# Batch 0 of a Fourier layer and a maxout layer on one core: the complex weight product by three products instead of four

## The chip, the core and the metric

The kernel runs on one core of one Trainium2 chip. The metric is the device time of one execution in microseconds (us). Before the change three runs took 1979.61, 1980.62 and 1983.82 us, median 1980.62. TensorE (PE) does the matmuls, VectorE (DVE) and ScalarE (ACT) the work between them, GpSimd (POOL) mostly issues DMAs, and SyncE (SP) only issues DMAs.

## The reference, cut to what matters

The input x has 8 batches of 3072 x 256. Each batch goes through a Fourier layer and then a maxout layer:

```python
X = np.fft.rfft(x, axis=1)                      # 3072 long
Yr = Xr @ w_r - Xi @ w_i + b_r                  # the complex product, 256 x 256
Yi = Xr @ w_i + Xi @ w_r + b_i
Y = soft_threshold(Yr) + 1j * soft_threshold(Yi)   # |.| - 0.01, not below 0
y = np.fft.irfft(Y, n=3072, axis=1)
h = np.maximum(np.maximum(y @ w1, y @ w2), y @ w3) # 256 -> 768
out = h @ w_out                                    # 768 -> 256
```

The maxout weights arrive as float64 and are turned into pairs of float16 numbers (a high and a low part) on the chip, with a common power of two that needs the largest magnitude of all of them.

## The kernel before, in words

The transform of length 3072 = 96 x 32 is done in two steps. A first product over 96 (`stage_a`, tile `pa`) writes to `a_d` in DRAM. Then come 12 groups, k = 0 to 11, each with four of the 48 pairs of frequencies: a second product over 32 (`stage_b`, tile `px`, result `t`), the complex weight product (`stage_w`, tile `py`, result `u`), the soft threshold, and the first product of the inverse (`stage_q`, tile `pz`, copied to `zs` and stored to `z_d`). When all 12 groups of a batch are in `z_d`, it is read back in eight chunks (`load_z`, tile `zq`) and the last inverse product (`pi`) and the maxout layer (`up`, tile `pu`; `down`, tile `pd`) follow.

Batches 1 to 7 are prepared while the maxout layer of the batch before them runs, in float16 pairs. Batch 0 has nothing to hide behind. It runs ahead of everything in plain float32 (`first_b`, `first_w`, `first_q`), in a loop k = -3 to 12 that does in this order: load `aj` of group k + 3, `first_b(k + 1)`, `first_w(k)`, `finish_w(k)`, `first_q(k - 1)` with its store, and then the items of `plan[k]`.

The plan prepares the maxout weights beside the groups. `load` brings a pair of tiles (SP), `largest` takes a maximum (DVE), `scale` finds the common exponent (DVE and a small matmul `pt`), and four phases `exponent`, `combine`, `join` and `finish` (DVE and ACT by turns, tiles `rw`, `ru`, `xhl`, `wuh`, `wul`, `woh`, `wol`) turn a tile into its float16 pair. `w_up` is the three input weights, `w_dn` is w_out. `w_dn.load(4)` is in `plan[6]`, `w_dn.largest(4)` and `w_dn.scale` in `plan[7]`. Later phases of other tiles are issued by `pump` from k = 8 on, and more behind the loop.

Every engine works through its instructions in a fixed order, which the compiler's scheduler chose: it follows the program, but puts an instruction ahead where its inputs are expected to be ready. So the plan's instructions stand between those of the groups, some before the program's place. SP issues `aj`, the weights, the tables and x's tiles in one queue; ACT issues `z_d` of batch 0 (L894); POOL issues `a_d`, the output, and `z_d` of other batches.

In `first_w` before the change `t` holds for each half j of the group (64 columns) the columns [-imag, real, imag]. Each half takes two products with w_r and two with w_i, over two blocks of the 256 inputs: 8 float32 matmuls of 128 x 256, with both halves' real and imaginary parts as rows 0 to 63 and 64 to 127. DVE adds the bias (L696), ACT makes the two one-sided parts (L701, L702), DVE subtracts them (L703). `first_q` needs the real rows of a half on partitions 0 to 63 and its imaginary rows on 64 to 127, which is how `u` lies. Group 11 has special frequencies and its own tables.

Of the kernel before, what the change touches and what calls it, by code (L numbers as in the profile page):

```python
# [101 lines left out]
def fourier_maxout_kernel(  # L102
# [131 lines left out]

    def load_fft_weights():
# [16 lines left out]
    def load_last_bias():  # L252
        rows = [b.rearrange("(r o d) -> r o d", r=1, o=1) for b in (b_r, b_i)]
        for c in range(2):
            nc.sync.dma_start(out=bias[64 * c:64 * c + 64, 1:2], in_=rows[c].broadcast_to([64, 1, D]))
        nc.gpsimd.dma_start(out=bias[96:97, 1:2], in_=rows[0])
# [53 lines left out]
    def scale_bias():  # L310
        mb = small("mxb")
        nc.vector.tensor_reduce(
            out=mb, in_=bias[:, 0], axis=AX.X, op=ALU.max, apply_absolute_value=True
# [191 lines left out]
    def load_m(q):  # L505
        b, q4 = divmod(q, NCH)
        xv = x[b].rearrange("(n1 n2) d -> n1 n2 d", n2=N2)[:, q4 * NQ:(q4 + 1) * NQ, :]
        with tc.issue_after(st["ld"].ins):
            st["m", q] = xm = fft.tile([N1, NQ * D], F32, name="xm", bufs=1)
# [148 lines left out]
    def first_b(k):  # L658
# [8 lines left out]
        st["t", k] = t = fft.tile([P, KD, 384], F32, name="tf", tag="t2", bufs=2)  # L667
        tv = t.rearrange("p h (j m) -> p (h j) m", j=2)
# [12 lines left out]

    def first_w(k):
        last = k == NJP - 1
# [3 lines left out]
        for j in range(2):  # L687
# [12 lines left out]
        t = fft.tile([P, 2, D], F32, name="t", bufs=1)  # L700
        nc.scalar.activation(out=t, in_=u, func=AF.Relu, bias=mlam)  # L701
        nc.scalar.activation(out=u, in_=u, func=AF.Relu, scale=-1.0, bias=mlam)  # L702
        nc.vector.tensor_tensor_reduce(  # L703
            out=u, in0=u, in1=t, scale=1.0, scalar=0.0, op0=ALU.subtract, op1=ALU.max,
            accum_out=mx[:, NJP + k:NJP + k + 1],
        )
# [4 lines left out]
        st["u", k] = u  # L711

    def first_q(k):
        u = st.pop(("v", k))
        pz = ff_tile("pz")
# [163 lines left out]
    def stage_q(k):  # L879
        b, kb = divmod(k, NJP)  # L880
        if b == 0 or plain(k):
# [11 lines left out]
            for q in range(2):  # L893
                nc.scalar.dma_start(  # L894
# [257 lines left out]
    for k in range(-3, NJP + 1):  # L1152
        for fn, i in (
            (load_a, k + 3), (stage_b, k + 1), (stage_w, k), (finish_w, k), (stage_q, k - 1),
        ):
            if 0 <= i < NJP:
                if fn == stage_q and i == NJP - 1:
# [4 lines left out]
        with tc.issue_after(st["ld"].ins):  # L1162
# [15 lines left out]
            if k == 6:  # L1178
                whole = ga_sb.rearrange("p i e n m -> p (i e n m)")
                nc.sync.dma_start(out=whole, in_=ga[:, 0:2 * N2 * N1])  # L1180
                first = fft.tile([N1, NQ * D], F32, name="xm", bufs=1).bitcast(F16)[:, 0:2 * NT]
# [8 lines left out]
    with tc.issue_after(st["late"].ins):  # L1190
        for c, v in enumerate((b_r, b_i)):
            row = v.rearrange("(o d) -> o d", o=1)
# [104 lines left out]
```

## Time and profile before

| | before |
|---|---|
| median of three runs | 1980.62 us |
| the profiled execution's own time | 1980.65 us |
| its span in the trace | 1978.9 us |
| PE busy over the span | 1961.3 us (99%) |
| DVE busy | 1521.3 us (77%) |
| ACT busy | 1064.3 us (54%) |
| POOL busy | 280.5 us (14%) |
| mean granted TensorE clock | 0.998 |

Busy time is the union of an engine's instructions; issuing a DMA is not counted as busy. A row of a timeline has its start, the time from the start of its first to the end of its last instruction, the engine, the line of the kernel, the operation, the tiles, and in square brackets the idle time of the engine before it and what ended that. Instructions of one engine overlap at their ends, so the step from one start to the next is what an instruction costs its engine. A float32 matmul stands as two records. Groups 0 to 11 of batch 0 lie between about 27 and 98 us of the span; the first maxout matmul starts at 110.78 us.

### The profile page before, as it was taken

How to read it: one execution, taken by the hardware profiler on the slowest of the kernel's cores; microseconds unless marked ns; L12 is line 12 of the kernel's file. 1: busy time of each engine (PE TensorE's matmuls, PEld its weight loads, DVE VectorE, ACT ScalarE, POOL GpSimd, SP SyncE). 2: the span in 40 equal slices, each digit the busy share in tenths (PEclk: the TensorE clock that was granted, in tenths of full speed). 3: DMA queues.
4: the chain of work that ended last, by engine and by line, in shares of the span. 5: the costliest groups of instructions: out<-in, count | busy, mean ns of one | idle time of the engine just before them, and what ended most of it. 6: DMA issues, size and time to landing. Idle time of an engine off the chain costs nothing.

```text
span 1978.9 us, 44328 instructions
## 1 busy us (share of the span) xinstructions
PE 1961.3 (99%) x16839; PEld 1355.9 (69%) x16839; DVE 1521.3 (77%) x3159; ACT 1064.3 (54%) x2186; POOL 280.5 (14%) x510
## 2 busy tenths in 40 slices
PE   9989999999999999999999999999999999999999
PEld 5746776676766766666766676666676677766666
DVE  3788887888877988778887888868887687765554
ACT  5755664566545565456554565545655455443343
POOL 1001111111111122111121021111122001100000
PEclk9999999999999999999999999999999999999999
DMA  8756564565545564555555465544552344221111
GB/s 291 212 150 172 157 163 124 156 174 154 145 133 163 143 189 115 151 150 161 159 137 149 133 186 145 147 139 130 149 154 73 90 115 123 68 76 49 49 49 33
DMA packets 201843, 269.75 MB, mean 136 GB/s; under 512 B 30846, under 2 KB 149982, under 8 KB 201534
## 3 DMA queue, kind: packets, MB, share of 16 engines
q1 hardware_dynamic: 168830, 191.37, 36.7%
q0 software_dynamic: 25168, 68.59, 10.7%
q10 hardware_dynamic: 7632, 6.95, 1.2%
q8 instruction: 133, 2.18, 0.5%
q14 instruction: 80, 0.66, 0.1%
HBM read 124.31 MB, written 75.50 MB: 101 GB/s over the span
## 4 chain that ended last, share of the span: by engine, by line
PE 93%; DVE 3%; DMA 2%; ACT 1%; issue 1%; SPq 0%; ACTq 0%; DVEq 0%
PE pu L179 19%; PE pu L181 18%; PE pu L180 18%; PE pd L181 6%; PE pd L180 6%; PE pd L179 6%; PE py L179 3%; PE py L180 3%; PE py L181 3%; PE pi L1021 2%; PE px L737 2%; PE pa L575 2%; PE pz L905 1%; PE pa L592 1%; PE py L692 0%
## 5 line engine op out<-in xcount | busy, mean ns | idle before, releaser
L179 PE MATMUL pu<-yh,wuh 128*128 128x384 f16 x2304 | 752.2, 327 | 2.6 <-DVE h L1062 1.7
L181 PE MATMUL pu<-yh,wul 128*128 128x384 f16 x2304 | 751.5, 326 | 0.0
L180 PE MATMUL pu<-yl,wuh 128*128 128x384 f16 x2304 | 751.5, 326 | 0.0
L173 ACT ACTIVATE hh<-h 128x384 f16<-128x384 f32 x384 | 200.2, 521 | 432.3 <-DVE h L1062 428.4
L181 PEld LDWEIGHTS <-wul 128*128 128x128 f16 x2304 | 225.5, 98 | 149.7 <-issue 0.9
L179 PEld LDWEIGHTS <-wuh 128*128 128x128 f16 x2304 | 225.3, 98 | 145.1 <-issue 34.2
L181 PE MATMUL pd<-woh,hh 128*128 128x256 f16 x1152 | 313.4, 273 | 0.7 <-DVE hh L174 0.7
L180 PE MATMUL pd<-wol,hh 128*128 128x256 f16 x1152 | 313.8, 273 | 0.0
L179 PE MATMUL pd<-woh,hh 128*128 128x256 f16 x1152 | 313.8, 273 | 0.0
L180 PEld LDWEIGHTS <-wuh 128*128 128x128 f16 x2304 | 225.5, 98 | 116.1 <-issue 5.0
L174 DVE SCALAR_TENSOR_TENSOR hh<-h,hh 128x384 f16<-128x384 f32 x384 | 213.3, 555 | 108.3 <-ACT hh L173 105.4
L1059 DVE TENSOR_TENSOR c<-pu,c 128x384 f32<-128x384 f32 x384 | 212.1, 552 | 95.8 <-PE pu L181 90.3
L1056 ACT ACTIVATE c<-pu 128x384 f32<-128x384 f32 x384 | 186.7, 486 | 139.9 <-PE pu L181 136.8
L1062 DVE TENSOR_TENSOR h<-pu,c 128x384 f32<-128x384 f32 x384 | 211.7, 551 | 29.2 <-PE pu L181 24.8
L1093 POOL DMA_DIRECT2D out_dram<-o x189 | 104.7, 559 | 581.3 <-ACT o L1091 569.7
L585 POOL DMA_DIRECT2D a_d<-aq x160 | 94.0, 591 | 612.4 <-ACT aq L582 590.0
L181 PE MATMUL py<-wch,tt 128*128 128x256 f16 x504 | 137.3, 273 | 0.0
L179 PE MATMUL py<-wch,tt 128*128 128x256 f16 x504 | 137.3, 272 | 0.0
L180 PE MATMUL py<-wcl,tt 128*128 128x256 f16 x504 | 137.3, 272 | 0.0
L179 PEld LDWEIGHTS <-hh 128*128 128x128 f16 x1152 | 112.7, 98 | 33.5
L180 PEld LDWEIGHTS <-hh 128*128 128x128 f16 x1152 | 112.7, 98 | 33.4
L181 PEld LDWEIGHTS <-hh 128*128 128x128 f16 x1152 | 112.7, 98 | 15.2 <-DVE hh L174 1.9
(236 smaller groups left out, 2659.3 us busy)
## 6 DMA issues: line engine op xcount, KB each, us to landing
zq<-z_d SPq DMA_DIRECT2D x63, 384.0 KB, 4.8
out_dram<-o POOLq DMA_DIRECT2D x189, 128.0 KB, 3.3
ab<-a_d SPq DMA_DIRECT2D x84, 256.0 KB, 4.1
ab<-ab SPq DMA_DIRECT2D x336, 64.0 KB, 3.0
vb<-vb SPq DMA_DIRECT2D x308, 64.0 KB, 2.9
z_d<-zs POOLq DMA_DIRECT2D x70, 256.0 KB, 3.8
xm<-in_x_dram SPq DMA_DIRECT2D x40, 384.0 KB, 3.5
a_d<-aq POOLq DMA_DIRECT2D x160, 96.0 KB, 2.9
```

The costliest lines, as they stand in the source:

```text
L173: nc.scalar.activation(out=hi, in_=src, func=AF.Copy, scale=scale)
L174: later(lambda: low(nc.vector.scalar_tensor_tensor(out=lo, in0=src, scalar=scale, in1=h, op0=ALU.mult, op1=ALU.subtract)))
L179: nc.tensor.matmul(o, lh, rh, start=start, stop=False, **kw)
L180: nc.tensor.matmul(o, lh, rl, start=False, stop=False, **kw)
L181: st["mm"] = nc.tensor.matmul(o, ll, rh, start=False, stop=stop, **kw)
L575: st["mm"] = nc.tensor.matmul(pa[r][64 * h:64 * h + 64], ft[rows, t], xt[rows, i, h], start=t == i, stop=t == 1,)
L585: nc.gpsimd.dma_start(out=av[1 - r, :, :, n:n + 512], in_=o[64 * h:64 * h + 48])
L737: nc.tensor.matmul(pv[:, h, :, g // 2, g % 2], ah[:, g // 2, g % 2, h * P:(h + 1) * P], mb_sb[:, i, 4 * kb + g].rearrange("p (c m) -> p c ...
L1056: st["act"] = nc.scalar.activation(out=c1, in_=p, func=AF.Copy)
L1059: st["dve"] = nc.vector.tensor_tensor(out=c1, in0=p, in1=c1, op=ALU.max)
L1062: st["dve"] = nc.vector.tensor_tensor(out=h32, in0=p, in1=st["c1"], op=ALU.max)
L1093: q.dma_start(out=out_v[b, c, t], in_=o)
```

## The change

For groups 0 to 10 the complex product is made by three products. With R and I the real and imaginary inputs, c = (R + I) w_r, then Yr = c - I (w_r + w_i) and Yi = c + R (w_i - w_r). `t` now holds R, I and their sum for all 128 frequencies of a group (ACT copies R and I, DVE adds them), the two sums of the weights are made once by DVE, and `first_w` becomes `quick_w`: 6 float32 matmuls of 128 x 256 in two PSUM tiles, a DVE addition of c and the bias (`bias_ri`, both biases side by side on all partitions), and a DVE addition of the other two products that also takes the maximum. The threshold is as before.

The result lies with real and imaginary parts side by side and 128 frequencies on the partitions, so four DMAs on SP of 64 rows each (64 KB) move the rows of `u` to `moved` in the order that `first_q` needs. `first_q` now runs two groups behind (`k - 2`, was `k - 1`); groups 10 and 11 both follow at k = 12. `z_d` of groups 0 to 9 is issued by POOL instead of ACT. `w_dn.largest(4)` and `w_dn.scale` stand in `plan[8]` instead of `plan[7]`. `bias_ri` is loaded early on SP in place of the first half of `bias`; its late load on POOL is gone. `moved` uses the buffers of `aq`, the weights' sums part of the tile `xm`.

```diff
+    spare_x = fft.tile([P, NQ * D], F32, name="xm", bufs=1)
+    sums = spare_x[:, 2 * D:4 * D].rearrange("p (k d) -> p k d", k=KD)
+    def sum_fft_weights(ws):
+        for kd, t in enumerate(ws):
+            r, i, s = (t[:, n * D:n * D + D] for n in range(3))
+            nc.vector.scalar_tensor_tensor(
+                out=sums[:, kd], in0=r, scalar=-1.0, in1=i, op0=ALU.mult, op1=ALU.subtract
+            )
+            nc.vector.tensor_tensor(out=s, in0=i, in1=r, op=ALU.subtract)
...
-            nc.sync.dma_start(out=bias[64 * c:64 * c + 64, 0:1], in_=rows[c].broadcast_to([64, 1, D]))
+            nc.sync.dma_start(out=bias_ri[:, c:c + 1], in_=rows[c].broadcast_to([P, 1, D]))
...
+        if k < NJP - 1:
+            pc = px.rearrange("p (h j c m) -> p h c j m", h=KD, j=2, c=2)
+            for c in range(2):
+                nc.scalar.activation(
+                    out=t[:, :, c * P:c * P + P].rearrange("p h (j m) -> p h j m", j=2), in_=pc[:, :, c],
+                    func=AF.Copy,
+                )
+            nc.vector.tensor_tensor(
+                out=t[:, :, 2 * P:3 * P], in0=t[:, :, 0:P], in1=t[:, :, P:2 * P], op=ALU.add
+            )
+            return
...
+    def quick_w(k):
+        t = st.pop(("t", k))
+        mx = batch(0, "u")
+        both = [ff_tile("py") for _ in range(2)]
+        for o, part, w in (
+            (both[0][:, 0:D], 2, [v[:, 0:D] for v in fft_weights]),
+            (both[1][:, 0:D], 1, [sums[:, h] for h in range(KD)]),
+            (both[1][:, D:2 * D], 0, [v[:, 2 * D:3 * D] for v in fft_weights]),
+        ):
+            for h in range(KD):
+                nc.tensor.matmul(
+                    o, t[:, h, part * P:(part + 1) * P], w[h], start=h == 0, stop=h == KD - 1
+                )
+        u = fft.tile([P, 2, D], F32, name="uf", tag="vh", bufs=3)
+        nc.vector.tensor_tensor(
+            out=u, in0=both[0][:, 0:D].rearrange("p (o d) -> p o d", o=1).broadcast_to([P, 2, D]),
+            in1=bias_ri, op=ALU.add,
+        )
+        nc.vector.tensor_tensor_reduce(
+            out=u, in0=both[1].rearrange("p (c d) -> p c d", c=2), in1=u, scale=1.0, scalar=0.0,
+            op0=ALU.add, op1=ALU.max, accum_out=mx[:, k:k + 1],
+        )
+        first_threshold(k, u)
+        if k % 2 == 0:
+            st["moved"] = fft.tile([P, NQ * D], F32, name="aq", bufs=2)
+        st["mv", k] = moved = st["moved"][:, k % 2 * 512:k % 2 * 512 + 512].rearrange("p (j d) -> p j d", j=2)
+        for c in range(2):
+            for j in range(2):
+                nc.sync.dma_start(out=moved[64 * c:64 * c + 64, j], in_=u[64 * j:64 * j + 64, c])
...
-                nc.scalar.dma_start(
+                (nc.gpsimd if k < NJP - 2 else nc.scalar).dma_start(
...
-    for k, n in ((4, 0), (5, 2), (5, 3), (7, 4)):
+    for k, n in ((4, 0), (5, 2), (5, 3), (8, 4)):
         planned(k, w_dn.largest, n)
-    planned(7, w_dn.scale)
+    planned(8, w_dn.scale)
...
-            (load_a, k + 3), (stage_b, k + 1), (stage_w, k), (finish_w, k), (stage_q, k - 1),
+            (load_a, k + 3), (stage_b, k + 1), (stage_w, k), (finish_w, k), (stage_q, k - 2),
+            (stage_q, NJP - 1 if k == NJP else -1),
```

## Rows read from the trace of the kernel before

**Rows 1.** The page's first two parts: busy time of the engines over the span, and DVE's busy share in 40 equal slices of 49.5 us (tenths, 9 is 90% or more).

```profile
span 1978.9 us, 44328 instructions
PE 1961.3 (99%) x16839; PEld 1355.9 (69%) x16839; DVE 1521.3 (77%) x3159; ACT 1064.3 (54%) x2186; POOL 280.5 (14%) x510
...
DVE  3788887888877988778887888868887687765554
```

**Rows 2.** Busy time by stretches: start and end, length, then busy us (and instructions) of PE, PEld, DVE, ACT and POOL, the granted clock, the mean busy share of the 16 DMA engines, and GB/s. The third row of stretches is from the bias addition of group 0 to that of group 11.

```profile
34.99:73.53 38.54, 36.90 (x187) 30.23 (x186) 34.58 (x85) 28.34 (x49) 0.49 (x1) 1.00 0.97 311
73.53:93.64 20.11, 20.11 (x99) 16.58 (x98) 15.42 (x42) 15.63 (x27) 1.54 (x5) 1.00 0.61 158
34.99:93.64 58.65, 57.01 (x285) 46.81 (x284) 50.00 (x125) 43.98 (x75) 2.03 (x6) 1.00 0.85 258
93.64:110.78 17.14, 13.13 (x53) 5.96 (x52) 8.89 (x24) 13.04 (x23) 2.67 (x5) 0.93 0.62 182
112.00:150.00 38.00, 34.99 (x234) 20.98 (x233) 36.24 (x72) 18.56 (x36) 0.51 (x1) 0.96 0.40 115
```

**Rows 3.** The chain that ended last, in order of time, through one group (start, us, what; each pair of records is one float32 matmul).

```profile
78.89 0.86 PE pz L718 x2
79.75 0.89 PE px L664 x8
80.64 0.43 PE py L691 x2
...
84.09 0.86 PE pz L718 x2
```

**Rows 4.** The one longer idle time of PE among the groups, and of DVE at the same place, from the timelines of the two engines.

```profile
73.22 1.10 PE L718 MATMUL pz<-uf,qf 128*128 128x512 f32 x2 [1.62 <-DVE col L265]
...
71.78 0.69 DVE L363 TENSOR_REDUCE mwd<-rw 128x2 f32<-128x512 f32 x1 [1.85 <-DMA rw<-in_moe_w_out_dram]
```

**Rows 5.** DVE's timeline: bias addition and threshold of groups 2 and 9 (L696, L703), and an addition of two SBUF tiles of 128 x 256 (L327) with its successor.

```profile
45.19 0.69 DVE L696 CUSTOM_DVE_ANT_1 uf<-py,bias 128x512 f32<-128x512 f32 x1
45.80 0.09 DVE L696 DVE_READ_ACCUMULATOR2_ANT mxu<- 128x1 f32 x1
...
48.88 0.68 DVE L703 CUSTOM_DVE_ANT_0 uf<-uf,t 128x512 f32<-128x512 f32 x1
...
84.13 0.69 DVE L696 CUSTOM_DVE_ANT_1 uf<-py,bias 128x512 f32<-128x512 f32 x1
...
87.00 0.69 DVE L703 CUSTOM_DVE_ANT_0 uf<-uf,t 128x512 f32<-128x512 f32 x1 [0.24 <-ACT uf L702]
...
130.04 0.41 DVE L327 TENSOR_TENSOR wst<-wst 128x256 f32<-128x256 f32 x1
130.37 1.27 DVE L137 SCALAR_TENSOR_TENSOR wcl<-wst,sc,wch 128x256 f16<-128x256 f32 x3
```

**Rows 6.** DVE's timeline: waits inside the stretch that no matmul ended, and the last work before the bias addition of group 11.

```profile
60.10 0.42 DVE L363 TENSOR_REDUCE mwd<-ru 128x1 f32<-128x256 f32 x1 [0.57 <-DMA ru<-in_moe_w_out_dram]
...
83.15 0.96 DVE L397 SCALAR_TENSOR_TENSOR xhl<-rw,xhl 128x768 uint32<-128x768 uint32 x1 [0.86 <-ACT xhl L393]
...
89.95 0.95 DVE L406 SCALAR_TENSOR_TENSOR rw<-rw 128x768 f32<-128x768 uint32 x1
90.94 0.99 DVE L409 TENSOR_TENSOR rw<-rw,xhl 128x768 f32<-128x768 f32 x1
91.96 0.56 DVE L390 TENSOR_SCALAR xhl<-rw 128x768 uint32<-128x768 uint32 x1
92.44 0.69 DVE L703 CUSTOM_DVE_ANT_0 uf<-uf,t 128x512 f32<-128x512 f32 x1
```

**Rows 7.** The page's DMA part, whole run: 64 KB moves within SBUF of other batches, and SP's timeline about its longest wait among the groups.

```profile
vb<-vb SPq DMA_DIRECT2D x308, 64.0 KB, 2.9
...
40.37 0.37 SPq L358 DMA_DIRECT2D rw<-in_moe_w_dram  x1
47.91 0.37 SPq L629 DMA_DIRECT2D aj<-a_d  x1
```

**Rows 8.** DMAs issued from 31 to 75 us: all packets, then tiles, queue, count, KB each and median us from issue to landing.

```profile
DMA packets 7791, 13.60 MB, mean 309 GB/s; under 512 B 663, under 2 KB 4853, under 8 KB 7691
...
aj<-a_d SPq DMA_DIRECT2D x10, 256.0 KB, 6.3
z_d<-zs ACTq DMA_DIRECT2D x12, 128.0 KB, 5.9
```

**Rows 9.** ACT's timeline of one group: the store of `z_d` (a DMA issue, ACTq) and the copy of `t` behind it.

```profile
47.16 1.25 ACTq L894 DMA_DIRECT2D z_d<-zs  x2
48.46 0.60 ACT L669 ACTIVATE tf<-px 128x512 f32<-128x512 f32 x1 [0.72 <-ACT uf L702]
```

**Rows 10.** The chain that ended last, from the bias addition of group 11 to the first maxout matmul.

```profile
93.64 0.69 DVE uf L696
...
97.33 1.13 PE pz L721 x4
...
107.29 0.62 ACT zh L173
...
110.78 0.80 PE pu L179 x2
```

More of the change, by code (lines that the diff above doesn't have):

```diff
@@ L254, in load_last_bias @@
         for c in range(2):
-            nc.sync.dma_start(out=bias[64 * c:64 * c + 64, 1:2], in_=rows[c].broadcast_to([64, 1, D]))
+            nc.sync.dma_start(out=bias[64 * c:64 * c + 64], in_=rows[c].broadcast_to([64, 2, D]))
         nc.gpsimd.dma_start(out=bias[96:97, 1:2], in_=rows[0])
@@ L312, in scale_bias @@
         nc.vector.tensor_reduce(
-            out=mb, in_=bias[:, 0], axis=AX.X, op=ALU.max, apply_absolute_value=True
+            out=mb, in_=bias_ri.rearrange("p c d -> p (c d)"), axis=AX.X, op=ALU.max, apply_absolute_value=True
         )
@@ L508, in load_m @@
         with tc.issue_after(st["ld"].ins):
-            st["m", q] = xm = fft.tile([N1, NQ * D], F32, name="xm", bufs=1)
+            st["m", q] = xm = fft.tile([P, NQ * D], F32, name="xm", bufs=1)[0:N1]
             nc.sync.dma_start(out=xm.rearrange("p (n d) -> p n d", n=NQ), in_=xv)
@@ L680, in first_b, with first_threshold @@
                 nc.gpsimd.memset(st["ts"][:, :, z:z + 1], 0.0)
+    def quick_w(k):
[27 more added lines that the diff above has]
+                nc.sync.dma_start(out=moved[64 * c:64 * c + 64, j], in_=u[64 * j:64 * j + 64, c])
+    def first_threshold(k, u):
+        t = fft.tile([P, 2, D], F32, name="t", bufs=1)
+        nc.scalar.activation(out=t, in_=u, func=AF.Relu, bias=mlam)
+        nc.scalar.activation(out=u, in_=u, func=AF.Relu, scale=-1.0, bias=mlam)
+        nc.vector.tensor_tensor_reduce(
+            out=u, in0=u, in1=t, scale=1.0, scalar=0.0, op0=ALU.subtract, op1=ALU.max,
+            accum_out=batch(0, "u")[:, NJP + k:NJP + k + 1],
+        )
+        st["u", k] = u
     def first_w(k):
+        if k < NJP - 1:
+            return quick_w(k)
         last = k == NJP - 1
@@ L699, in first_w @@
         )
[L700 to L706, printed above, removed]
+        first_threshold(k, u)
         if last:
@@ L1153, in fourier_maxout_kernel @@
         for fn, i in (
[L1154 removed]
+            (load_a, k + 3), (stage_b, k + 1), (stage_w, k), (finish_w, k), (stage_q, k - 2),
+            (stage_q, NJP - 1 if k == NJP else -1),
         ):
             if 0 <= i < NJP:
+                if fn == stage_w and i == 0:
+                    sum_fft_weights(fft_weights)
                 if fn == stage_q and i == NJP - 1:
@@ L1180, in fourier_maxout_kernel @@
                 nc.sync.dma_start(out=whole, in_=ga[:, 0:2 * N2 * N1])
-                first = fft.tile([N1, NQ * D], F32, name="xm", bufs=1).bitcast(F16)[:, 0:2 * NT]
+                first = spare_x[0:N1].bitcast(F16)[:, 0:2 * NT]
                 nc.sync.dma_start(out=first, in_=ga[:, 2 * N2 * N1:])
@@ L1189, in fourier_maxout_kernel @@
                 pump()
-    with tc.issue_after(st["late"].ins):
-        for c, v in enumerate((b_r, b_i)):
-            row = v.rearrange("(o d) -> o d", o=1)
-            nc.gpsimd.dma_start(out=bias_ri[:, c], in_=row.broadcast_to([P, D]))
     quiet = st["power"].ins, st["zs"].ins
```

2 lines of the change are left out of this document (1 added, 1 removed).

## The prediction

> **What bounds the kernel now.** I read the busy times first, then the stretches of batch 0, then the chain of waits through them, and last the timelines of DVE, ACT and SP there. Over the whole span PE is busy 99% and DVE 77%, and DVE is at seven to eight tenths until late in the span [rows 1]. So every us counts in which PE works or stands still, and the change touches only the stretch in which batch 0's groups are made. That stretch runs from the bias addition of group 0 at 34.99 us to that of group 11 at 93.64, 58.65 us for eleven steps. PE is busy 57.01 of it, always at the full granted clock, but DVE is busy 50.00 too, and in its first 38.54 us DVE has 34.58 (90%) and the DMA engines 97% [rows 2]. The reader is to see three resources near their limits there, not one. Only behind 73.53 us does PE stand alone, with DVE at 15.42 of 20.11 and the DMA engines at 61%.
>
> Within a group the chain shows a period of 5.20 us (84.09 - 78.89): 0.86 for `pz`, 0.89 for `px`, and eight float32 matmuls of 0.43 for `py` [rows 3]. The one longer idle time of PE is 1.62 us at 73.22: DVE stood 1.85 us waiting for w_out's last load, with its maximum in front of a threshold that PE needed [rows 4].
>
> **The change part by part.**
>
> *Two matmuls fewer in each of groups 0 to 10.* 22 x 0.43 = 9.5 us off PE [rows 3]. Of these, the ten groups that lie behind the bias addition of group 0 and group 0 itself all count on PE's side: a period becomes 5.20 - 0.87 = 4.33 us. With PE alone, the 58.65 us would become 58.65 - 9.5 - 1.6 (the stall) = 47.5 us.
>
> *Work added to DVE.* The bias addition was one instruction with a step of 0.61 us (45.80 - 45.19); now two of that size stand in its place, since the plain addition also reads 128 x 512 from PSUM. The sum of R and I is an addition of two tiles in SBUF, 128 x 256, with a step of 0.33 (130.37 - 130.04) [rows 5]. That is 0.61 + 0.33 = 0.94 us in each of groups 1 to 10 and 0.61 in group 0 behind its first addition: 9.4 + 0.6 = 10.0 us. The four sums of weights (4 x 0.33 = 1.3 us) fall ahead of 34.99 and the wider maximum of the bias is 0.3 us; I take these at 0 because DVE still waits there for tables and first products; without that cover they cost up to 1.6 us once. DVE's work in the stretch is then 50.00 + 10.0 = 60.0 us, more than the 58.65 that the stretch has now and far more than PE's 47.5. DVE takes over as the bound.
>
> How long the stretch gets depends on what of DVE's work must lie in it. Waits that no matmul ended, 0.57 for a load and 0.86 for ACT [rows 6], remain or go with ACT's relief (below); I keep 1.0 us. Against that, the weight phases at 89.95, 90.94 and 91.96 (0.95 + 0.99 + 0.56 = 2.5 us) feed nothing that the last groups need [rows 6] and can fall behind group 11, where DVE has 8.89 of 17.14 us busy [rows 2]. So 60.0 + 1.0 - 2.5 = 58.5 us against 58.65: -0.15 us. The ends: if all weight work stays in front and all waits remain, 60.0 + 1.4 + 1.6 = 63.0 (+4.4 us); if about 11 us of it fall behind, PE's 47.5 us (-11.1). I take the value near the middle, nearest to the present order, in which the plan's phases stand among the groups; DVE has 34.58 of 38.54 us in the first part with that order.
>
> *The moves and the lag of two groups.* Four DMAs of 64 KB per group on SP, each behind the threshold. The four issues are 0.37 each [rows 7], 1.5 us. From the end of a `py` (where the bias addition starts) to the end of the threshold takes 49.56 - 45.19 = 4.4 us in group 2 and 87.69 - 84.13 = 3.6 in group 9 [rows 5]. The landing isn't in the trace for this tile. Lower end: 2.9 us, the same size and kind in other batches [rows 7]; upper end: 6.3 us, what `aj` takes on the same queue in this crowded stretch [rows 8]. `pz` now comes two periods behind its `py`, so a period can't be below half of this sum: (4.4 + 1.5 + 6.3) / 2 = 6.1 us in the crowd, (3.6 + 1.5 + 2.9) / 2 = 4.0 behind it. With 4.6, the middle of the two ends, it is 5.25 in the crowd, which is today's period. So the moves alone also allow about no gain up to 73 us, and they need no term beside DVE's; above 4.6 they do (second rival). Behind the moves on SP wait the next `aj`, weight and table loads. SP today has waits as long as 7.2 us between two loads (40.37 + 0.37 to 47.91) [rows 7] and PE runs on, since `aj` is fetched three groups ahead; I take 0.
>
> A page speaks against these moves. The Trainium skill, SBUF — State Buffer, section Door 1: The DMA port swizzle, says that a transfer to partitions 0 to 63 or 64 to 127 reaches only half of the ports, and that its measured rate was 196 GB/s where 128 rows had 328. By that figure four moves take an estimated 1.3 us on the wire in place of 0.8, half a microsecond per group. No row here shows a transfer of 64 rows against one of 128 at equal load; the sum above is by the landing times of the rows.
>
> *`z_d` from POOL.* ACT loses 1.25 us of issuing per group [rows 9], and its copies of `t` shrink. ACT is busy 28.34 of 38.54 us [rows 2], and seven stores of 1.25 beside that made it 37, so this is real relief, but ACT isn't what bounds the changed stretch: it removes DVE's waits for ACT, counted above. POOL is idle (2.03 us busy of 58.65), and nobody waits for these stores until the read-back behind group 11: 0.
>
> *w_out's maximum one group later.* PE's 1.62 us stall goes in the PE sum. In a DVE-bound stretch it is worth DVE's 1.85 us wait at most, which I have left out of the waits kept. If the load comes no sooner than today, the same wait stands one group later.
>
> *The end of the stretch.* Today `pz` of group 11 starts at 97.33 [rows 10]. Now `pz` of group 10 stands in front of it and needs its moves: the threshold of group 10 ends at 93.13 [rows 6], plus 1.5 of issues and 2.9 of landing (the DMA engines are less busy there) is 97.5, plus 0.86 of matmul: `pz` of group 11 starts at 98.4, +1.0 us. The read-back waits for both. The chain from there to the first maxout matmul (107.29 `zh`, 110.78 `pu`) stays.
>
> *Sum.* -0.15 + 1.0 = +0.9; against it stands that the kept wait of 0.86 for ACT probably goes with ACT's relief: +0.0 us. The profiled execution took 1980.65 us, 1.75 more than its span, and lies at the median of the three (1980.62). I predict 1980.7 us: no change that can be measured. A measurement of this kernel tells about 0.2% (4 us) from no change, so same means 1976.7 to 1984.6.
>
> **The rivals.**
>
> *PE stays the bound and the weights' phases fall behind (faster).* The scheduler may set the groups' instructions first, since in program order a group stands ahead of its own plan items. Then the stretch shrinks towards 47.5 us. For it: behind 73.53 us DVE has 4.7 us idle, and between groups 11 and the first `pu` 8.25 more [rows 2]. Against it: from 112 to 150 us DVE is busy 36.24 of 38.00 and PE idle 3.0 [rows 2], so what doesn't fit into those 8.25 us is paid there. With 11.1 us gained on PE, 10.0 + 2 of DVE work to place, 8.25 taken free and the rest (about 4) paid, and +1.0 at the end: -11.1 + 4 + 1.0 = -6, 1974.6 us. With all of it hidden 1970.6.
>
> *The moves come too late (slower).* One mechanism, on SP and the DMA engines up to about 75 us: `pz` waits for rows that queue behind loads. 13.60 MB went in 44 us at 309 GB/s [rows 8], and the moves add seven times 256 KB, 1.8 MB or 5.9 us of that traffic. At a landing of 6.3 us the period is 6.1 against 38.54 / 7 = 5.5 us now, stall included: 7 x 0.6 = +4.2 us, and the crowd lasts longer: one more group at 6.1, not 5.2, is +0.9. Behind it three groups gain 0.87 each, -2.6; the spilled traffic delays the weight loads by up to 5.9 us, of which I count half, +3.0; the end +1.0. Together +6.5: 1987.2 us. It decides from a landing of 5.1 us on (2 x 5.5 - 5.9). For it: `aj` and `z_d` at 6.3 and 5.9; against it: 2.9 for such moves elsewhere, and `z_d`'s traffic is on another queue now.
>
> **How the numbers follow.** Forecast, DVE as the bound: 0.44, own range 1976 to 1985. PE as the bound: 0.34, 1970 to 1977. Moves too late: 0.22, 1983 to 1990. The range that holds 8 in 10 reaches into both rivals, 1971 to 1987. Faster gets nearly all of the second case and a little of the first, 0.37; slower most of the third and a little of the first, 0.23; same 0.40.
>
> **What would show it.** On the right track: `py` with six matmuls and 4.3 us of PE work per group; DVE busy over 95% from group 0 to 11, with the bias addition of group 11 at 92 to 96 us; `pz` waiting for DVE, not for a DMA; moves landing in 3 to 5 us; `pz` of group 10 just ahead of that of group 11. Wrong: group 11 below 90 us with the phases L406 to L409 behind it, or `pz` released by the moves' DMA through most groups with the period above 5.5.

## The result and the profile after

The changed kernel takes 1995.53 us, the median of four runs (1993.20 to 1999.34); the kernel before took 1981.74 beside it (1979.61 to 1983.82). The ratio is 1.0073 with a 95% interval of 1.0055 to 1.009: 13.8 us slower, outside the predicted range of 1971 to 1987. The profiled execution took 1999.34 us with a span of 1997.5; 2.1 us of what it lies above its median were lost ahead of group 0, whose first `px` starts at 29.42 us where it starts at 27.3 to 28.0 in most profiles of this kernel and its variants. Stretches below therefore start at the first `px`.

Almost all of the loss lies in batch 0's groups; behind the first maxout matmul `pu` the profile is 2.4 us longer than the one before (1997.5 - 126.96 against 1978.9 - 110.78). The two stretches from the first `px` to the first `pu`, in the view by stretches (start and end, length, then busy us and instructions of PE, PEld, DVE, ACT and POOL, the granted clock, the DMA share, GB/s); before:

```profile
27.28:110.78 83.50, 76.16 (x369) 57.86 (x370) 61.60 (x157) 59.35 (x104) 4.71 (x11) 0.98 0.81 247
```

After, the same stretch, and the one from group 0's bias addition to group 11's, which answers to the third row of [rows 2]:

```profile
29.42:126.96 97.54, 75.93 (x324) 53.43 (x325) 72.66 (x183) 57.48 (x103) 15.76 (x29) 0.91 0.81 240
...
37.24:105.50 68.26, 54.43 (x246) 40.96 (x245) 60.02 (x149) 43.01 (x77) 11.98 (x22) 0.95 0.85 250
```

The stretch is 14.0 us longer. PE has 45 records fewer, which is the 22 matmuls that the change saves (two records each; a few records can be missing), and yet it is busy just as long, 75.93 us against 76.16: what remains runs at a lower granted clock, 0.91 against 0.98. Its idle time goes from 83.50 - 76.16 = 7.3 to 97.54 - 75.93 = 21.6 us, +14.3. So the 9.5 us that were saved don't show in PE's busy time, and the idle time is the loss. The clock takes a part of them; that it takes all is not shown, since e4 below has the matmuls of before at a clock of 0.97, and PE is busy 80.36 us in it. What ended the idle times (engine, instruction, what it waited for: us in total, times, longest), after, 28 to 128 us:

```profile
PE pz L776 <- DMA aq<-uf: 5.9, 5, 1.8
PE pt L278 <- DVE col L276: 3.8, 2, 2.3
PE pi L179 <- ACT zh L173: 3.4, 1, 3.4
PE px L675 <- DMA aj<-a_d: 3.2, 2, 3.0
PE py L714 <- ACT tf L682: 2.2, 1, 2.2
PE py L714 <- DVE xm L241: 2.1, 1, 2.1
PE pz L779 <- DVE mxu L738: 0.7, 1, 0.7
```

There is no single wait. Rows that were moved (`aq`), a weights' maximum (`col`), `aj`, ACT and DVE all come late by turns. The wait for `zh` was 2.4 us before as well, and the one for `xm` is for the sums of the weights. What the first-named three share, 12.9 of these 21.3 us, is seen on SP (start, us, engine, line, tiles); after, with five lines of its issues to 75 us:

```profile
41.23 2.49 SPq L732 DMA_DIRECT2D aq<-uf  x4
43.82 0.53 SPq L369 DMA_DIRECT2D rw<-in_moe_w_dram  x1
...
55.74 2.39 SPq L732 DMA_DIRECT2D aq<-uf  x4
58.17 0.59 SPq L369 DMA_DIRECT2D rw<-in_moe_w_dram  x1
58.87 0.44 SPq L640 DMA_DIRECT2D aj<-a_d  x1
```

In the kernel before, the fifth load of `w_up` was issued at 40.37 us [rows 7]; here it is the one at 58.17. Four moves cost SP 2.4 us to issue (0.6 each), stand behind the threshold, and everything else of the queue stands behind them: the `aj` issued at 58.87 landed at 65.0, and PE waited 3.0 us for it. w_up's maximum is complete (its `col`) at 71.6 us instead of 55.2, w_out's at 89.4 instead of 73.0, and x's tiles for the next batch, which SP asked for from 66.70 us on, are asked for from 93.17 on.

It is not that more was moved in that time: DMAs issued from 31 to 75 us, after (all packets; tiles, queue, count, KB each, median us to landing), against 13.60 MB at 309 GB/s [rows 8]:

```profile
DMA packets 7298, 11.51 MB, mean 262 GB/s; under 512 B 836, under 2 KB 4804, under 8 KB 7294
...
aj<-a_d SPq DMA_DIRECT2D x7, 256.0 KB, 7.1
...
aq<-uf SPq DMA_DIRECT2D x20, 64.0 KB, 2.6
```

Behind 73 us, where groups had a period of 5.20 us [rows 3], PE's timeline of one group is now (start, us, instruction, idle time before it and what ended it):

```profile
76.87 1.10 PE L776 MATMUL pz<-aq,qf 128*128 128x512 f32 x2 [0.83 <-DMA aq<-uf]
77.95 1.13 PE L714 MATMUL py<-xm,tf 128*128 128x256 f32 x4
78.92 1.46 PE L714 MATMUL py<-wst,tf 128*128 128x256 f32 x6
80.21 1.05 PE L675 MATMUL px<-mb_all,aj 128*128 128x128 f32 x8
81.11 0.60 PE L714 MATMUL py<-wst,tf 128*128 128x256 f32 x2
82.47 1.12 PE L776 MATMUL pz<-aq,qf 128*128 128x512 f32 x2 [0.76 <-DMA aq<-uf]
```

It has six `py` (twelve records) in place of eight, and the step from `pz` to `pz` is 5.60 us, ended by the moved rows.

The clock, by stretches, after:

```profile
35.00:40.00 5.00, 5.00 (x21) 4.28 (x20) 3.92 (x15) 2.45 (x7) 0.00 (x0) 0.75 1.02 390
40.00:45.00 5.00, 2.76 (x15) 2.36 (x14) 4.56 (x15) 2.84 (x6) 0.00 (x0) 0.93 0.56 178
45.00:50.00 5.00, 5.00 (x21) 4.16 (x21) 4.15 (x9) 3.69 (x8) 0.00 (x0) 0.73 0.88 251
...
65.00:70.00 5.00, 4.97 (x18) 3.83 (x18) 3.95 (x11) 2.05 (x4) 0.51 (x1) 0.68 0.59 213
```

PE is busy all of 45 to 50 us and is granted 0.73 in the mean, so a good part of it at the lower of the two levels (1.2 and 2.4 GHz); in the five us before, it stood idle for 2.2. In the same way 65 to 70 us follow the 3.0 us wait for `aj`. In [rows 2] the clock is 1.00 from 34.99 to 93.64. So these stalls cost more than their length. Not every stall does: behind the 2.29 us wait for `col` that ended at 89.73 us the clock is 1.00 from 90 to 95 us, and in e4 below it is 1.00 in every five us from 30 to 105, with waits of up to 2.1 us. What decides is not shown.

The end of the chain, after, which answers to [rows 10] (start, us, what):

```profile
105.59 0.60 DVE uf L760
...
108.59 1.52 PE pz L779 x4
...
112.24 1.09 PE pz L776 x2
...
123.77 0.62 ACT zh L173
...
127.03 0.73 PE pu L179 x2
```

Group 11's `pz` comes 11.3 us later than before (97.33), and from it to the first `pu` take 18.4 us instead of 13.5. Group 10's `pz` stands behind it, not ahead of it as I had expected, and so do all of x's products `pa`, of which the first (94.30 and 95.98 us) stood ahead of it before.

### The profile page after: what moved, and what is told of

Read it like the earlier page. It is cut to its first block, busy times and chain, and to the rows that moved or that the text cites. A ratio compares the mean times of both kernels' runs of the same rounds, so it can differ in the third digit from the quotient of the medians.

```text
span 1997.5 us, 44396 instructions
## 1 busy us (share of the span) xinstructions
PE 1962.8 (98%) x16795; PEld 1352.2 (68%) x16795; DVE 1532.4 (77%) x3185; ACT 1063.1 (53%) x2186; POOL 291.6 (15%) x528
## 4 chain that ended last, share of the span: by engine, by line
PE 89%; DVE 4%; DMA 3%; ACT 2%; issue 1%; SPq 0%; ACTq 0%; POOL 0%; DVEq 0%; POOLq 0%
PE pu L179 18%; PE pu L180 18%; PE pu L181 18%; PE pd L181 6%; PE pd L180 6%; PE pd L179 6%; PE py L179 3%; PE py L180 3%; PE py L181 3%; PE pi L1079 2%; PE px L795 2%; PE pa L586 1%; PE pz L963 1%; PE pa L603 1%; DMA ab<-ab 1%
## 5 line engine op out<-in xcount | busy, mean ns | idle before, releaser
L174 DVE SCALAR_TENSOR_TENSOR hh<-h,hh 128x384 f16<-128x384 f32 x384 | 213.2, 555 | 109.1 <-ACT hh L173 106.3
```

The lines of the kernel that those rows point to most:

```text
L174: later(lambda: low(nc.vector.scalar_tensor_tensor(out=lo, in0=src, scalar=scale, in1=h, op0=ALU.mult, op1=ALU.subtract)))
```

## The experiments

Each median stands beside its own runs of the kernel before, between 1980.3 and 1982.5 us; ratios are with 95% intervals. The columns are from each kernel's profiled execution (us): w_up's and w_out's maxima complete (`col`), group 11's maximum (`col` behind its threshold), first `pu`.

| kernel | w_up | w_out | group 11 | `pu` | median | ratio |
|---|---|---|---|---|---|---|
| before | 55.2 | 73.0 | 97.3 | 110.8 | 1981.7 | 1 |
| changed | 71.6 | 89.4 | 108.5 | 127.0 | 1995.5 | 1.0073 [1.0055, 1.009] |
| e1 changed, no moves | 61.2 | 84.0 | 98.8 | 112.0 | 1986.3 | 1.0019 [1.001, 1.0029] |
| e7 e1, no additions | 64.7 | 83.6 | 101.1 | 115.7 | 1985.0 | 1.0015 [1.0003, 1.0027] |
| e10 e7, `aj` earlier | 61.8 | 80.0 | 94.6 | 108.4 | 1983.1 | 1.0004 [0.9993, 1.0016] |
| e15 e7, `aj` earlier from group 0 | 61.1 | 80.6 | 94.3 | 110.4 | 1982.4 | 1.001 [1.0001, 1.002] |
| e4 before, unread moves | 70.5 | 85.0 | 107.2 | 123.7 | 1994.1 | 1.0062 [1.0045, 1.0079] |
| e5 the same without the wait | 68.6 | 84.7 | 106.3 | 120.5 | 1991.3 | 1.0048 [1.0031, 1.0065] |
| e6 before, one row behind the wait | 62.4 | 78.6 | 103.7 | 117.1 | 1985.9 | 1.0023 [1.0013, 1.0032] |
| e2 moves on GpSimd | 62.2 | 95.1 | 114.9 | 130.6 | 2005.2 | 1.0111 [1.0094, 1.0127] |
| e3 moves on ScalarE | 68.8 | 98.6 | 123.2 | 138.5 | 2010.1 | 1.0137 [1.0121, 1.0152] |
| e12 changed, `aj` earlier | 66.2 | 85.5 | 102.7 | 120.2 | 1996.7 | 1.008 [1.0057, 1.0103] |
| e13 moves behind the loads | 66.6 | 83.3 | 106.9 | 125.0 | 1995.7 | 1.0079 [1.0064, 1.0094] |
| e14 moves one group later | 65.2 | 85.1 | 104.1 | 123.8 | 1995.4 | 1.0077 [1.006, 1.0094] |

Single profiles scatter by some us about their medians (e12's was the fastest of its four runs, by 5 us; e7's the slowest of ten, 6 us above its median), so the medians decide and the columns show where.

**The moves taken away, and the moves alone.** e1 is the changed kernel without the moves (`pz` reads `u` as it lies); e4 is the kernel before with moves that nobody reads.

```diff
@@ e1, quick_w @@
-        for c in range(2):
-            for j in range(2):
-                nc.sync.dma_start(out=moved[64 * c:64 * c + 64, j], in_=u[64 * j:64 * j + 64, c])
@@ e4, first_w of the kernel before @@
+        if not last:
...
+            for c in range(2):
+                for j in range(2):
+                    nc.sync.dma_start(out=moved[64 * c:64 * c + 64, j], in_=u[64 * j:64 * j + 64, c])
```

> The changed kernel without the moves of u's rows: first_q reads u as it lies, so batch 0's part of the output is not the reference's; all else as in the change, the lag of two groups too. Theory A (the moves stand on SP's queue in front of the loads, and what SP waits for delays weights and aj): the loads come as early as before, PE's waits for maxima and aj shrink to those of before, and the matmuls saved show: 1973 to 1979 us. Theory B (pz waits for its rows, the lag is too short): the 5.9 us of PE's waits for aq go and little else, with the clock's share some 8 us: 1986 to 1990. Theory C (DVE's added work is the bound): nothing is taken from DVE, 1990 to 1996.

> The kernel before with the same four moves on SP in groups 0 to 10 and nobody who reads the moved rows. Theory A: the moves alone delay the loads: 1986 to 1994 us. Theory B (nobody waits for the rows) and theory C (DVE has no more to do): within 3 us of the kernel before.

Without moves the changed kernel loses 3.9 us, with them 13.8; its time lies where theory B had it and not where A had it, so the moves are not the whole loss. The moves alone, in the kernel before, lose 11.6, although nobody reads their rows, as theory A had it and B did not. e4's stretch from first `px` to first `pu`:

```profile
27.50:123.68 96.18, 80.36 (x368) 57.68 (x369) 62.04 (x157) 59.67 (x104) 4.59 (x11) 0.97 0.87 245
```

and its largest wait of PE in it:

```profile
PE px L664 <- DMA aj<-a_d: 7.4, 7, 2.1
```

The kernel before waited 1.2 us for `aj`. So the moves cost some 10 us by what they do to other transfers. Neither the moved rows being late nor a lower clock is needed for it (the 0.97 comes from behind 105 us). One wait does hang on the moved rows without reading them: `aq` is also the buffer of x's products, and ACT waits 3.8 us for it once, up to 110.18 us.

**The wait and the traffic apart.** e5 moves rows of the weights instead of `u`, so that SP waits for nothing of the group; e6 leaves one row of 1 KB behind the threshold. Both are the kernel before otherwise, and nobody reads what is moved.

```diff
@@ e5, in place of e4's line @@
+                    nc.sync.dma_start(out=moved[64 * c:64 * c + 64, j], in_=fft_weights[c][64 * j:64 * j + 64, 0:D])
@@ e6, in place of e4's four @@
+            nc.sync.dma_start(out=moved[0:1, 0], in_=u[0:1, 0])
```

> The kernel before with four moves of 64 KB per group on SP that copy rows of the loaded weights, so that they wait for no threshold, and that nobody reads. They cost SP's issues and the DMA engines' bytes as in the moves of u (which took 11.6 us here), but no wait. If the wait for the threshold on SP's queue is the price (theory A), this is within 3 us of the kernel before; if the bytes and the issues are (theory D), 1989 to 1996 us.

> The kernel before with one DMA per group on SP that copies one row of u behind the threshold and that nobody reads: the wait is that of the moves, the bytes and three of four issues are gone. Theory A: 6 to 12 us slower than the kernel before, 1988 to 1994. Theory D: within 3 us of it.

Four moves without the wait cost 9.7 us, the wait with one issue and one row 4.3; together (e4) 11.6. The two overlap, and by the medians the larger part is the four DMAs themselves (the intervals of the two ratios just touch). e5 lies where theory D had it, e6 between the two expectations. 40 to 60 us of the kernel before:

```profile
40.00:60.00 20.00, 19.97 (x103) 16.64 (x103) 19.14 (x42) 15.08 (x26) 0.49 (x1) 1.00 0.95 327
```

and of e5:

```profile
40.00:60.00 20.00, 19.56 (x94) 14.74 (x92) 15.43 (x29) 13.82 (x25) 0.00 (x0) 1.00 0.91 259
```

The 16 DMA engines are nearly as busy (0.91 against 0.95), and move 259 GB/s instead of 327. Over the whole stretch they are busy 0.81 x 83.50 = 67.6 us before and 0.87 x 96.18 = 83.7 in e4, for 245 x 96.18 - 247 x 83.50 = 2.9 MB more (44 moves of 64 KB are 2.9 MB): 5.5 us for each MB of moves, against 67.6 / 20.6 = 3.3 for the mean MB before. By the changed kernel against e1 (0.81 x 97.54 = 79.0 and 0.79 x 84.42 = 66.7 us for 2.8 MB more) it is 4.4. All of the added busy time is put to the moves here, and the shares have two digits, which is some 0.5 us in each product. The stretches of e1, e5 and e6:

```profile
27.55:111.97 84.42, 70.33 (x325) 51.03 (x326) 71.24 (x183) 57.22 (x103) 15.55 (x29) 0.97 0.79 244
...
27.50:120.51 93.01, 79.28 (x368) 56.82 (x369) 61.67 (x157) 59.83 (x104) 4.69 (x11) 0.99 0.88 254
...
27.40:117.05 89.65, 77.27 (x368) 57.68 (x369) 60.66 (x157) 60.15 (x104) 7.85 (x11) 0.99 0.79 232
```

Without the wait (e5) the DMA engines are busy 0.88 x 93.01 = 81.8 us, 14 more than before; with the wait and one row (e6) 0.79 x 89.65 = 70.8, 3 more. If SP's issues were the price and not the transfers, the engines should stand idler, as in e6. That speaks for the transfers, but no run has one without the other.

The Trainium skill, SBUF — State Buffer, section Door 1: The DMA port swizzle, on which the prediction drew, gives 196 GB/s for 64 rows against 328 for 128, at 1 MiB. That points the same way; no run here has 128-row moves of the same bytes.

**Other queues, other places.** e2 and e3 issue the moves from GpSimd and ScalarE. e13 leaves them on SP but behind the loads planned for their group, e14 behind the next group's `aj` as well; e12 asks for `aj` one group earlier.

```diff
@@ e2 (e3: nc.scalar) @@
-                nc.sync.dma_start(out=moved[64 * c:64 * c + 64, j], in_=u[64 * j:64 * j + 64, c])
+                nc.gpsimd.dma_start(out=moved[64 * c:64 * c + 64, j], in_=u[64 * j:64 * j + 64, c])
@@ e13, e14: the four issues become a function @@
+        st["moves"] = moves
@@ e13, behind the items of plan[k] @@
+            st.pop("moves", lambda: None)()
@@ e14, behind load_a of the next k @@
+                if fn == load_a:
+                    st.pop("moves", lambda: None)()
@@ e12 @@
+    load_a(0)
-            (load_a, k + 3), (stage_b, k + 1), (stage_w, k), (finish_w, k), (stage_q, k - 2),
+            (load_a, k + 4), (stage_b, k + 1), (stage_w, k), (finish_w, k), (stage_q, k - 2),
```

> The changed kernel with the four moves of a group issued by GpSimd instead of SP. Theory A: SP's loads go out as before, 1976 to 1984 us. Theory B: the rows land no sooner behind GpSimd's issues, pz still waits for them, 1990 to 1996. Theory C: 1990 to 1996.

> The changed kernel with the four moves issued by ACT. They wait on ACT's queue for the threshold and take some 2.4 us of ACT per group. Theory A: SP's loads are early, weights' maxima too, but ACT's own work stands behind the waits: 1982 to 1990 us. Theory B and theory C: 1992 or more.

> The changed kernel whole, with each aj of batch 0 asked for one group earlier. Theory A (the loss is in the main the order of SP's queue: aj behind the moves, then low clock behind the stalls): PE's waits for aj (3.2 us) go, but the weights' rows still come late behind the moves: 1991 to 1994, 2 to 4 us less than the changed kernel. Rival B (the lost time is DVE's or ScalarE's chain through a group, and aj is only late because it may be): 1995 to 1997. Rival C (the weights' rows pushed still further back decide): above 1997.

> The changed kernel whole; the four moves of a group are issued on SP behind the weights' and tables' loads that are planned for that group instead of ahead of them. Theory A (the place in SP's order is the cost: the wait for the threshold and the issues hold the loads back): 1986 to 1990, w_up's last rows asked for before 55 us and its maximum's col before 62 us (71.6 in the changed kernel). Rival B (the moves' issues, bytes and landings cost by themselves wherever they stand): 1994 to 1997. Rival C (the moves now come late, because the queue waits on a load's buffer ahead of them, and pz waits for them): above 1998, pz waiting for aq more than 10 us.

> The changed kernel whole; the four moves of a group are issued on SP one group later, behind the aj that is asked for then, so that SP need not wait for the threshold. Theory A (order and wait are the cost): 1985 to 1988, SP's waits for the threshold under 3 us in all. Rival B (the issues and bytes cost by themselves): 1992 to 1996. Rival C (now pz waits for rows that are too late): above 1998, with pz's waits for aq above 10 us.

On other engines the moves are worse: 22.8 and 27.7 us lost, e2 beyond all its expectations, with `pz` waiting 13.5 and 12.3 us for its rows. On SP these other places gain nothing: the medians of e12, e13 and e14 lie within 1.2 us of the changed kernel's, and their ratios are no better. e14's waits of PE, 27 to 130 us:

```profile
PE pt L278 <- DVE col L276: 7.1, 2, 5.2
...
PE px L675 <- DMA aj<-a_d: 1.1, 2, 0.6
PE pz L780 <- DMA aq<-uf: 0.5, 2, 0.3
```

`pz`'s waits for rows are gone (5.9 to 0.5 us), those for `aj` fell from 3.2 to 1.1, and the time is the same: PE now stands at the weights' exponent, whose maximum still comes 10 us later than before. The rival of rows that come too late fell here. My theory that the order on SP was the cost lost its forecast (1985 to 1990), but it was not put to the test that I meant: SP's largest wait in e14, 28 to 112 us, is still for the threshold,

```profile
SPq L734 <- DVE mxu L742: 14.4, 5, 4.9
```

where I had expected under 3 us, and the changed kernel has 9.9 by that line. What the wait costs is told by e6 and e5, not by these. A run with e14's order and `aj` earlier from group 0 on (e16) gave 1.0085 [1.0068, 1.0102], no better and slower than all that was expected of it.

> The changed kernel whole; moves one group later behind the aj, and aj asked for one group earlier from group 0 on. Theory A (SP's order is the cost of the moves, aj's lateness that of the products): 1981 to 1985. Rival B (moves and DVE's additions cost by themselves): 1990 to 1996. Rival C (no difference to the variant with the moves one group later alone): within 1 us of that.

**Loads on a queue of their own.** e17 gives batch 0's loads of weights, `ga` and the next x to GpSimd (and the stores of z back to ScalarE), so that SP has only `aj`, moves and small tables; e18 does it to the kernel before.

```diff
-            nc.sync.dma_start(out=raw, in_=self.parts[n][3])
+            nc.gpsimd.dma_start(out=raw, in_=self.parts[n][3])
...
-            nc.sync.dma_start(out=xq.rearrange("p (n d) -> p n d", n=NQ), in_=xv)
+            (nc.gpsimd if NCH <= q < EARLY else nc.sync).dma_start(out=xq.rearrange("p (n d) -> p n d", n=NQ), in_=xv)
```

> The changed kernel whole, with batch 0's loads of the weights' rows, of ga and of the next batch's x issued by GpSimd, the z_d stores by ScalarE again, so that on SP only aj, the moves and the small tables are left. Theory A (the loads behind the moves on SP are late, and that is the loss): w_up's column at 55 to 63 us, first pu at 110 to 116, 1981 to 1988. Rival B (the moves cost by bytes and landings): first pu above 121, 1992 to 1997. Rival C (GpSimd's queue holds the loads as long as SP's did): as e18 says of the kernel before.

> The kernel before with the same loads issued by GpSimd. Theory A (SP was no bound in the kernel before): 1980 to 1984, w_up's column at 55 to 60 us. Rival B (SP's waits for z_d, 13 us behind aj in the kernel before, held loads back, and a queue of their own gains): 1974 to 1979. Rival C (GpSimd's issues are slower and hold up its own stores of a): above 1985.

Both are far slower, 1.0156 [1.0125, 1.0187] and 1.0094 [1.0074, 1.0115]; e17 lies outside all its expectations, e18 in the last of its own (above 1985). GpSimd's loads of w_up in e18 (timeline from 28 us; with one cut off there they are six, from 26.62 us on):

```profile
27.35 3.55 POOL L358 DMA_DIRECT2D rw<-in_moe_w_dram  x5
```

and what PE waited for then, in e18:

```profile
PE px L664 <- DMA aj<-a_d: 10.1, 1, 10.1
```

A queue with nothing ahead of it asked for six weights' loads of 768 KB within 4.3 us, and the first `aj` (11.5 us to landing) and the Fourier weights (15.5 us and more) shared the bandwidth with them. A part of the wait is what that last expectation names: w_out's rows and `xm` were asked for from 1.32 us on, the last store of `a_d` left at 24.63 us instead of 20.62, and the first `aj` was asked for at 29.51 instead of 24.43. In the kernel before, SP's order is also the order in which the groups get bandwidth. These two runs don't tell issues from bytes. e17 against e18, 14.4 us, has the products, the moves and some other differences in it.

**The products without the moves.** e7 is e1 without the sum of R and I and without the first product's addition; e10 and e15 also ask for `aj` one group earlier (e15 from group 0 on only).

```diff
-            nc.vector.tensor_tensor(
-                out=t[:, :, 2 * P:3 * P], in0=t[:, :, 0:P], in1=t[:, :, P:2 * P], op=ALU.add
-            )
...
-            (both[0][:, 0:D], 2, [v[:, 0:D] for v in fft_weights]),
+            (both[0][:, 0:D], 0, [v[:, 0:D] for v in fft_weights]),
...
-            out=u, in0=both[1].rearrange("p (c d) -> p c d", c=2), in1=u, scale=1.0, scalar=0.0,
+            out=u, in0=both[1].rearrange("p (c d) -> p c d", c=2), in1=bias_ri, scale=1.0, scalar=0.0,
@@ e15 (e10: as e12) @@
+            (load_a, k + 3 if k < 1 else k + 4), (load_a, 4 if k == 0 else -1),
```

> The changed kernel without the moves, and without what it added to DVE in each group: the sum of R and I is left out (the first product takes R in its place) and so is the addition of the first product, so batch 0's part of the output is not the reference's. Six matmuls per group stay. Theory C (DVE's additions ate the gain of the matmuls): 1972 to 1979 us, 8 to 12 below the version without moves (1986.3). If something else holds that version (the lag, the stores by GpSimd, the order), 1984 to 1988.

> The three products without the moves, without the sum of R and I and without the first product's addition (batch 0's values are not the reference's), as run before at 1985.0 us, now with each aj asked for one group earlier. Theory A (with six matmuls a group PE waits for aj, 3.4 us, and for the low clock behind these waits): 1979 to 1982, and PE's waits for aj under 1 us. Rival B (in 30 to 58 us the 16 DMA engines are full at .99 and 400 GB/s, so that no earlier issue makes aj land earlier; whatever is asked for earlier only moves what is late): 1984 to 1987, with the DMA share at .95 or more to 58 us and PE's waits moved to another load. Rival C (ScalarE's copies of t are the bound of a group): 1984 to 1986, with py's waits for ACT tf above 4 us and those for aj gone.

> The three products without the moves, without the sum of R and I and without the first product's addition (batch 0's values are not the reference's), with aj asked for one group earlier from group 0 on only. Theory A (aj and the start take the gain of the saved matmuls): 1975 to 1979, first pu at 104 to 107. Rival B (DMA share near 1 and the low granted clock behind short stalls take it): 1981 to 1984. Rival C (group 0's start, the sums of the weights on DVE, takes 2 us and the rest is lost after batch 0, where px waits for ab): first pu at 106 to 109, 1980 to 1983, PE idle over 2.5 us in 200 to 400 us.

Even with 9.5 us of matmuls and 10 us of DVE's additions gone, none is faster than the kernel before; e7 and e15 lie where a rival had them that keeps the gain away, e10 between two expectations. Group 0's bias addition to group 11's, in e1:

```profile
34.80:95.43 60.63, 52.43 (x246) 41.02 (x245) 57.02 (x145) 42.54 (x77) 12.45 (x24) 0.97 0.81 255
```

and in e15:

```profile
36.30:90.10 53.80, 49.96 (x242) 40.06 (x240) 49.07 (x127) 40.88 (x74) 12.52 (x22) 0.97 0.83 268
```

With the additions DVE is busy 94% of the stretch, close to the over 95% of the forecast; without them and with `aj` earlier the stretch does shrink, by 4.8 us against 58.65 [rows 2] (e7, without `aj` earlier, has 59.30, from 38.49 to 97.79 us in its slow profile). But it starts 1.3 us later, and of the 3.5 us that group 11 is earlier, 3.1 are gone at the first `pu` (110.4 against 110.8). e15's whole stretch against the first row above:

```profile
27.30:110.40 83.10, 70.49 (x325) 51.79 (x326) 62.35 (x161) 56.93 (x104) 16.37 (x29) 0.94 0.79 249
```

PE is busy 5.7 us less, not 9.5, at a clock of 0.94, and idle 5.3 us more. Its waits are short and for everyone: 3.6 us for ACT's copies, 2.3 for `aj`, 1.9 for a threshold, 1.5 for a maximum. What would have to be removed to collect the saved matmuls is open.

A part of the loss is not among the groups at all. From the first `pu` to the end of its span the kernel before takes 1868.1 us; e1, e7, e10 and e15 take 1871.0 to 1873.6, more than all other profiles (1865.9 to 1870.5). So e1's first `pu` is only 1.2 us late and its span 5.0 us longer, and e10 leads by 2.3 us at the first `pu` and has lost it by the end. One wait of PE that grew, e10, whole run (0.2 us before behind the first `pu`):

```profile
PE px L782 <- DMA ab<-ab: 3.9, 6, 1.9
```

`ab` holds rows of later batches; why they are late there is not shown. Asking for `aj` earlier brings perhaps 1 to 2 us here, with intervals that overlap, and nothing in the kernel before (e11, 1.0008 [0.9996, 1.0021]).

> The kernel before, with each aj of batch 0 asked for one group earlier (the load of group k+4 in place of k+3; five buffers as before). Theory A (before, aj arrives in time but for 1.2 us of px waits): 1980.5 to 1982.5, no change that can be told. Rival B (aj one group earlier keeps a buffer of the ring longer or pushes weights' rows back on SP, so that w_out's maximum is later): 1983 to 1986.

**The small parts alone.** w_out's maximum and exponent one group later in the kernel before (e8), and its z stored by GpSimd (e9):

```diff
@@ e8, and w_dn.scale in plan[8] @@
-    for k, n in ((4, 0), (5, 2), (5, 3), (7, 4)):
+    for k, n in ((4, 0), (5, 2), (5, 3), (8, 4)):
@@ e9 @@
-                nc.scalar.dma_start(
+                (nc.gpsimd if k < NJP - 2 else nc.scalar).dma_start(
```

> The kernel before with w_out's last maximum and its exponent one group later and nothing else. PE's 1.6 us stall at that place goes if the load is there by then: 0 to 2 us faster than the kernel before; if the wait only shifts by a group, no difference. Theory A and C say nothing of it.

> The kernel before, with one edit of the change alone: the z_d stores of groups 0 to 9 are issued by GpSimd instead of ScalarE. Theory A (the stores' queue plays no part in the loss): 1982 us, within 2 us, and the first pu at 110.8 within 1 us. Rival B (the stores on the other queue take DMA bandwidth earlier or later and hold aj back; part of the 3.9 us by which the variant without moves is slower): 1983.5 to 1985. Rival C (the 1.25 us of ScalarE's issue per pair of stores was a cost in the kernel before): 1978 to 1980, with the copies of t earlier.

1.0002 [0.9992, 1.0011] and 1.0004 [0.9994, 1.0015]: neither does anything that can be told. The profile of e9, some 3 us above its median, has w_up's maximum 5.7 us later than before and no wait of PE for it, so a late maximum alone is no cost until PE comes to it.

## Why the prediction was wrong

**The step that failed** is the one on the moves and the queue: "So the moves alone also allow about no gain up to 73 us, and they need no term beside DVE's", and behind it, of what waits on SP, "I take 0". The term is 13.8 - 3.9 = 9.9 us by e1 against the changed kernel, and 11.6 by e4. The working looked at the moves as a latency between a threshold and its `pz`, and latency was right enough: they land after 3.0 us in the median (4.6 taken; 2.9 to 6.3 as ends). But it priced nothing of what they take from others. The row that should have given a term was in the prediction: DMA engines 97% busy in the first 38.54 us [rows 2]. The second rival worked it out as 5.9 us of traffic; I put that into a rival only, and made it depend on landings above 5.1 us. By the DMA engines' busy time it is 8 to 10 us for that rival's seven groups (12 to 16 for all eleven), since these bytes are dearer than the mean.

**The issues** were taken at 0.37 us, 1.5 a group; they are 0.59 in the median and 2.4 to 4.8 a group. The 0.37 was a load's; the trace before has 308 moves of the same size, `vb<-vb`, with 0.605 in the median. The 7.2 us gap on SP [rows 7] showed that nothing was late then; I read it as room in the queue, but SP stood in a wait there (7.1 us, for a store of `z_d` by the profile). With the wait for the threshold and one row of traffic, the kernel loses 4.3 us (e6).

**DVE's work** was about right: 60.0 us predicted, 60.02 measured in the stretch of 68.26, though the agreement to 0.02 is luck (e1, with the same additions, has 57.02); additions have steps of 0.60 (99.38 to 99.98 us), as taken. But it fills 88% and not over 95%, so DVE isn't what bounds the changed kernel. Where the moves are away (e1) it nearly is: 57.02 of 60.63 us against the 58.5 predicted for the stretch, and group 11's `pz` starts at 98.78 us where I had 98.4. So for the groups of the kernel without the moves the forecast is about right, with the first `pu` 1.2 us late; of e1's loss of 3.9 us the rest lies behind that and had no term. The larger part of the error is the moves. With the additions away (e7) only some 0.5 us come back (a loss of 3.4 against 3.9), so DVE as the one bound is too simple there too: ACT, `aj` and the clock stand close behind it (e15's waits).

**PE's side.** The 47.5 us took 22 matmuls off a stretch that holds 20 of them, since group 0's lie ahead of it; that makes 48.4 and changes no case. The clock had no term; it was 1.00 in the whole stretch before [rows 2], and I took 0.43 for every matmul. Behind some stalls of 2 to 3 us it fell, and PE's busy time stayed where it was, with 22 matmuls fewer. The moves' cost doesn't need it: e4 loses 11.6 us with 1.00 among the groups.

**The rivals.** Faster, 1974.6: excluded by e7 and e15, which have no additions on DVE and still aren't faster. Slower, 1987.2: the right sign and in part the right place (SP and the DMA engines to 75 us), but not its mechanism. Landings stayed under its own deciding point of 5.1 us in the median (3.0, the longest 6.9), and in e14 `pz` waits only 0.5 us for its rows without a gain. Its 3.0 us for delayed weights' loads was the part nearest to what happened: w_up's maximum came 16.4 us later (71.6 against 55.2).

**The parts taken at 0**: z's stores and w_out's maximum are 0 (e9, e8). The sums of the weights, 0 to 1.6 us, show as a wait of `py` of 2.1 us once (DVE `xm`).

**What stays open**: how the moves' cost divides between the four issues on SP and the bytes on the DMA engines, for which their busy time speaks. Four one-row copies, or one copy of 128 rows, would tell; neither was tried. Nor is it settled why the products gain nothing without moves; the lag of two groups was not run alone.

## What to carry to other kernels

When a change adds transfers to a stretch where the DMA engines are near full, price the bytes and the issues first and the landing time last; the cheap test is the old kernel with the new transfers and no reader. A queue that carries loads for later work is a schedule: a wait put into it moves every later load, and a free queue in its place can starve the first ones. Work taken off a full engine is gained only if what stands next behind it, and the clock after some of the new stalls, let it through; a variant with the saving and without its costs (e7) shows that before the costs are argued about.

## What was not expected of the hardware

The moves of 64 rows, SBUF to SBUF, raised the DMA engines' busy time by 4.4 to 5.5 us per MB, where the mean MB of this stretch takes 3.3. Issuing one costs SP 0.59 us in the median, no less than a weights' load of 768 KB (0.37 to 0.66 before). The granted clock, 1.00 through 58 us of float32 matmuls, fell to 0.68 to 0.75 over 5 us behind single stalls of 2 to 3 us, with PE busy all of those 5 us, but stayed at 1.00 behind another of 2.29 us.
